# Seven block products for eight in the gate projection of the last four token groups

## The chip, the cores and the metric

The kernel runs on one core of a Trainium2 chip. The metric is device time in microseconds (us) of one execution. Executions of one kernel agree to about 0.3%. No execution here was in a slow state: the granted TensorE clock was between 0.996 and 1.0 in every profiled one. TensorE is called PE in the profile, its weight loads PEld, VectorE DVE, ScalarE ACT, GpSimd POOL and SyncE SP. A profiled span is some 1.8 us shorter than the time of the same execution.

## The reference

Cosine-weighted linear attention over 8 batches, 8 heads, 576 positions and 64 dimensions, then a gated feed-forward block over the resulting 4608 tokens of 512 features:

```python
def _attn_ref(q, k, v):
    # cos_w, sin_w: one number for each position
    def phi(x, c, s):
        r = np.maximum(x, 0.0)
        return np.concatenate([r * c, r * s], axis=-1)
    q_p, k_p = phi(q, cos_w, sin_w), phi(k, cos_w, sin_w)
    kv = np.einsum('bhsf,bhsd->bhfd', k_p, v)
    z = np.sum(k_p, axis=2)
    num = np.einsum('bhsf,bhfd->bhsd', q_p, kv)
    den = np.einsum('bhsf,bhf->bhs', q_p, z)[..., None] + 1e-06
    return num / den

def _moe_ref(x, w_gate, w_val, w_out):      # 4608x512, 512x1536, 512x1536, 1536x512
    g = x @ w_gate
    silu = g * (1.0 / (1.0 + np.exp(-g)))
    val = x @ w_val
    return silu * val @ w_out
```

The change touches `x @ w_gate` only.

## The kernel before

The tokens are handled in nine groups of 512, numbered 0 to 8. A group's projections run chunk by chunk, 12 chunks of 128 of the 1536 hidden features. In each chunk TensorE computes gate and value (4 + 4 products of 512 columns), ScalarE the silu, VectorE the product of the two. TensorE's results go to PSUM, a memory that the kernel handles as eight banks:

```python
    def ffn_mm(tg, fc, lo=0, hi=GH, which=(0, 1)):
        # cut: two PSUM banks, one for gate, one for value
        for i in which:
            for kc in range(KC):        # KC = 4
                nc.tensor.matmul(out=st["f", tg, fc, lo][i], lhsT=(wg_sb, wv_sb)[i][:, kc, fs],
                                 rhs=xT[tg][:, ts, kc], start=(kc == 0), stop=(kc == KC - 1))

    def ffn_silu(tg, fc, ...):
        nc.scalar.activation(out=sg[:, 0:n], in_=st["f", tg, fc, lo][0], func=AF.Silu, scale=DOWN)

    def ffn_mul(tg, fc, ...):
        nc.vector.tensor_tensor(out=ht[:, fc, r:r + n], in0=sg[:, 0:n], in1=ps[1], op=ALU.mult)
```

Behind each chunk stands a slot, into which the attention work for later groups is put: tiles of x of the next group (a TensorE product, then three VectorE steps, then a transposing DMA), table products of queries and values, key-value products. In the traces below VectorE works through its instructions in the order in which the program issues them.

```python
    for t in range(2 * OUT, NTG * OUT):          # tiles of x of groups 2 to 8
        # cut
            at(s, lambda t=t: a_tile2(t), turn(t))   # products, den, rec, x on VectorE; DMA transpose to xT
    for tg in range(1, NTG):
        s0 = SLOTS * tg
        for fc in range(FC):                     # FC = 12 chunks
            ffn_fc(tg, fc)
            if tg > 1:
                sums_behind(fc)                  # sums of tokens for the output, on VectorE
            slot(s0 + fc)
        if tg > 1:
            out_by_quarters(tg, lambda i: slot(s0 + FC + i))
```

`out_by_quarters` is the output projection, and already a block scheme: hidden features and tokens are split in halves, and seven products of half-size blocks stand in for eight, at the price of sums and differences of blocks on VectorE. The key-value result goes from PSUM to SBUF in four copies of one phase, two by ScalarE, two by VectorE:

```python
    def kv_out2(b):
        # cut
        for w, eng in enumerate((nc.scalar.copy, nc.vector.tensor_copy)):
            for i in range(2):
                eng(out=kv2s[b % 2][w * D:(w + 1) * D, :, :, i], in_=ps[i * D:(i + 1) * D, :, :, w])
```

Of the kernel before, what the change touches and what calls it, by code (L numbers as in the profile page):

```python
# [18 lines left out]
def kernel(  # L19
# [10 lines left out]
    nc = tc.nc  # L30
# [17 lines left out]
    HC = FC // 2  # L48
    HT = T // 2
    HD = d_model // 2  # L50

    consts = ctx.enter_context(tc.tile_pool(name="consts", bufs=1))
    raw = ctx.enter_context(tc.tile_pool(name="raw", bufs=3))
    rel = ctx.enter_context(tc.tile_pool(name="rel", bufs=1))
    phip = ctx.enter_context(tc.tile_pool(name="phip", bufs=2))
    xp = ctx.enter_context(tc.tile_pool(name="xp", bufs=4))
    xtp = ctx.enter_context(tc.tile_pool(name="xtp", bufs=3))
    smp = ctx.enter_context(tc.tile_pool(name="smp", bufs=3))
    sgp = ctx.enter_context(tc.tile_pool(name="sgp", bufs=5))
    obp = ctx.enter_context(tc.tile_pool(name="obp", bufs=2))  # L60
    psum = ctx.enter_context(tc.tile_pool(name="psum", bufs=1, space=bass.MemoryType.PSUM))

# [6 lines left out]
    held = {}  # L69

    filled = [False] * 8

    def take(n, hold=None, fills=False, seeded=False):

        taken = {x for r in held.values() for x in r}
        free = [b for b in range(0, 8, n) if not any(b <= x < b + n for x in taken)
                and (filled[b] or not seeded)]

        b0 = min(free, key=lambda b: (n == 1 and hold is not None and hold[0] == "o" and b ^ 1 not in taken,
                                      sorted(used[b:b + n], reverse=True)))  # L80
        if hold is not None:
            held[hold] = range(b0, b0 + n)
        filled[b0:b0 + n] = [fills or seeded] * n
        touch(range(b0, b0 + n))
        return banks[:, b0] if n == 1 else banks[:, b0:b0 + n]
# [15 lines left out]

    def raw_of(b, nm):
        if (b, nm) not in raws:
            raws[b, nm] = raw.tile([P, G, NC, D], BF16, name=f"raw_{nm}")
        return raws[b, nm]

    def load(b, nm, parts=1):
# [48 lines left out]
    ident = consts.tile([P, P], BF16)  # L156
    make_identity(nc, ident)
    kvd = []
    for j in range(2):
        t = consts.tile([P, 8 * J * D1], BF16, name=f"kvd_{j}")  # L160
        if j:
            nc.gpsimd.memset(t.bitcast(FP32), 0.0)
        kvd.append(t.rearrange("p (e j w i x) -> p e j w i x", e=2, j=J, w=2, i=2))


    zeros = consts.tile([P, P], BF16)
# [41 lines left out]
        in_=csk.rearrange("p c e -> p (c e)").to_broadcast([P, NC * 2, D]),  # L208
    )
    v2s = []  # L210
    for j in range(2):
        t = consts.tile([P, G, NC, 2, W], BF16, name=f"v2_{j}")
        nc.vector.tensor_copy(out=t[:, :, :, :, D], in_=csk.unsqueeze(1).to_broadcast([P, G, NC, 2]))
        v2s.append(t)


    wg_sb = consts.tile([P, KC, d_ff], BF16)
    wv_sb = consts.tile([P, KC, d_ff], BF16)
    wg_r = moe_w_gate.rearrange("(c p) f -> p c f", p=P)
    wv_r = moe_w_val.rearrange("(c p) f -> p c f", p=P)  # L220
    wo_r = moe_w_out.rearrange("(c p) f -> p c f", p=P)
# [35 lines left out]

    def vmul(b, g):
        nc.vector.tensor_tensor(  # L259
            out=v2s[b % 2][:, g, :, :, 0:D],  # L260
            in0=(first if b == 0 and g == 0 else {"v": raw_of(b, "v")})["v"][:, g].unsqueeze(2).to_broadcast([P, NC, 2, D]),
            in1=tab, op=ALU.mult,
        )
# [34 lines left out]
    def kv_mm(b):  # L298
        ps = st[b, "kvps"] = take(2, ("kv", b))
        for j, c in [(j, c) for j in range(J) for c in range(NC)]:  # L300
            for i in range(2):
                for e in range(2):
                    es = slice(e * SH, (e + 1) * SH)
                    g = 2 * j + i
                    nc.tensor.matmul(  # L305
                        out=ps[i * D:(i + 1) * D, e, j * 2 * D1:(j + 1) * 2 * D1],
                        lhsT=raws[b, "k"][es, g, c],
                        rhs=v2s[b % 2][es, g, c, :, 0:D1],
                        start=(c == 0), stop=(c == NC - 1),
                    )  # L310

# [47 lines left out]
            give_back(("kvf", j))  # L359


    qf = consts.tile([P, 2, J, 2, D], BF16)
    qr = [lodge(4 * J * SH, BF16).rearrange("p (e j c s) -> p e j c s", e=2, j=J, c=2) for i in range(2)]
    qwT = [lodge(8 * J * SH, BF16).rearrange("p (w e j c s) -> p w e j c s", w=2, e=2, j=J, c=2) for i in range(2)]

# [68 lines left out]
    def x_rec(t, ps, ys=slice(0, 4)):  # L434
        if ys.start == 0:
            st["rec", t] = smp.tile([P, H, 1], FP32, name="rec")
            st["x", t] = xp.tile([P, d_model], BF16, name="x")
        nc.vector.reciprocal(out=st["rec", t].rearrange("p (e y) o -> p e y o", e=2)[:, :, ys],
                             in_=st["den", t].rearrange("p (e y) o -> p e y o", e=2)[:, :, ys])

# [40 lines left out]
    def x_norm(t):  # L481
        num = st.pop(("num", t)).rearrange("p j e (i x) -> p (j e i) x", i=2)
        den = smp.tile([P, H, 1], FP32, name="den")
        nc.vector.tensor_scalar(out=den, in0=num[:, :, D:D1], scalar1=1e-6, scalar2=DOWN,
                                op0=ALU.add, op1=ALU.mult)
        rec = smp.tile([P, H, 1], FP32, name="rec")
        nc.vector.reciprocal(out=rec, in_=den)
        x = xp.tile([P, d_model], BF16, name="x")
        for j in range(J):
            hs = slice(4 * j, 4 * j + 4)  # L490
            nc.vector.tensor_tensor(
                out=x[:, 4 * j * D:(4 * j + 4) * D].rearrange("p (i e d) -> p e i d", i=2, e=2),
                in0=num[:, hs, 0:D].rearrange("p (e i) d -> p e i d", e=2),
                in1=rec[:, hs].rearrange("p (e i) o -> p e i o", e=2).to_broadcast([P, 2, 2, D]), op=ALU.mult,
            )
        st["x", t] = x

    def xT_of(t):
        tg, off = divmod(t, GH // 2)
        if tg not in xT:  # L500
            xT[tg] = xtp.tile([P, GH // 2, KC, P], BF16, name="xT")
        return xT[tg][:, off]

    def x_turn_pe(t, ks=slice(0, KC)):
        ps = take(1, ("xt", t, ks.start)).bitcast(BF16).rearrange("p (k x) -> p k x", x=P)
        for kc in range(ks.start, ks.stop):
            nc.tensor.transpose(out=ps[:, kc], in_=st["x", t][:, kc * P:(kc + 1) * P], identity=ident)  # L507
        st["xt", t, ks.start] = ps[:, ks]

    def x_turned(t, eng, ks=slice(0, KC)):  # L510
# [40 lines left out]
    def ffn_act(*a):  # L551
        ffn_silu(*a)
        ffn_mul(*a)

    def ffn_fc(*a):

        ffn_mm(*a)
        ffn_act(*a)

    out_v = out.rearrange("(b p c) f -> b c p f", p=SH, c=NC)  # L560
    o_ps = {}
# [68 lines left out]
    def out_by_quarters(tg, slot_of):  # L630
# [60 lines left out]
        if last:  # L691
            store_two(t0 + 2, slice(HD, d_model))
        product(c, aq[:, 1, 1], T4, False)
        copied("dve", C21, c)
        free("c")
        if last:
            store_two(t0 + 2, slice(0, HD))
# [175 lines left out]
        load_kv(3)  # L873


    for b in range(2, B):
        s0 = SLOTS * (b - 1)
        keng = "dve" if b == 2 else "act"
        steps = [lambda b=b, g=g: phi_q(b, g) for g in range(G)]
        steps += [lambda b=b, g=g: (relu_k(b, g, g + 1, keng), vmul(b, g)) for g in range(G)]  # L880
        if b == 2:
            fs, tq = [s0 + i for i in (0, 0, 1, 1, 4, 5, 5, 6)], (s0 + 2, s0 + 2)
        else:
            p0 = s0 - SLOTS
            fs, tq = [p0 + 12, p0 + 12] + [p0 + 11 + i for i in range(2, 8)], (p0 + 15, p0 + 16)
            if b == 3:
                fs, tq = [p0 + 12 + i for i in range(4)] + [s0 + 4, s0 + 4, s0 + 5, s0 + 5], (s0 + 2, s0 + 2)
            at(p0 + 3 if b < 5 else p0 + 1, lambda b=b: load_behind(b))
        tk = (s0 + 4, s0 + {2: 8, 3: 7}.get(b, 5))
        for s, f in zip(fs, steps):  # L890
            at(s, f)
        for e in range(2):
            at(tq[e], lambda b=b, e=e: qturn_dma(b, e))
        at(tk[-1], lambda b=b: kv_mm(b), lambda b=b: kv_out2(b))
        at(tk[-1] + 1, lambda b=b: kv_free(b))
    for t in range(2 * OUT, NTG * OUT):
        tg, i = divmod(t, OUT)
        s = SLOTS * (tg - 1) + (5 if tg > 2 else 4) + 2 * i
        if t == 2 * OUT:
            at(s, a_(t, 0))  # L900
            at(s + 1, a_(t, 1), turn(t))
        elif tg == 2:
            at((9, 10, 11)[i - 1] + SLOTS, lambda t=t: a_tile2(t), turn(t))
            if i == 2:
                at(11 + SLOTS, load_3)
        else:
            if t in (13, 14, 15):
                s = SLOTS * 2 + t - 4
            at(s, lambda t=t: a_tile2(t), turn(t))
    for tg in range(1, NTG):  # L910
        s0 = SLOTS * tg
        for fc in range(FC):
            ffn_fc(tg, fc)
            if tg > 1:
                sums_behind(fc)
# [3 lines that stand above are left out]
            continue  # L919
        for i in range(OUT):  # L920
            ffn_out(tg * OUT + i)
            weight_sum(i)
            slot(s0 + FC + i)
# [31 lines left out]
```

## Time and profile before

| | before |
|---|---|
| time, median of the 4 runs beside the changed kernel | 318.05 us (317.81 to 318.79) |
| profiled span | 316.2 us |
| busy: TensorE / VectorE / ScalarE | 309.1 / 220.2 / 134.1 us |
| group 5, from its first gate product to that of group 6 | 32.39 us |
| group 6 / group 7, in the same way | 32.43 / 30.92 us |
| group 8, projections / output to the end of the span | 20.72 / 13.96 us |

The prediction below shows the lines of the page and the table of stretches. One more view is needed: the waits of TensorE by cause. Each line names the waiting engine, tile and line, what it waited for, then the microseconds in total, the number of times and the longest.

```profile
PE banks L172 <- DVE zeros L167: 1.0, 1, 1.0
PE banks L401 <- DVE wt_sb L389: 0.6, 1, 0.6
PE banks L376 <- DVE qf L368: 0.4, 1, 0.4
PE banks L535 <- DMA xT<-x: 0.2, 1, 0.2
```

Three of the four are at the start of the program; from the steady groups on there is one wait of 0.2 us. There is no idle time of TensorE left to remove, only work.

### The profile page before, as it was taken

To read this page: it belongs to the slowest core of one execution; us is meant where nothing else is said; L and a number is where in the kernel's file an instruction comes from. 1 tells how busy PE (TensorE), PEld (TensorE's weight loads), DVE (VectorE), ACT (ScalarE), POOL (GpSimd) and SP (SyncE) were. 2 spreads that over 40 slices of the span, in tenths; PEclk is the share of its full clock that TensorE was granted. 3 is DMA by queue.
4 is the path that set the end of the run, shared out by engine and by line. 5 is a ranking of instruction groups with operands and counts; after the bars stand their busy time and mean duration, and the time that the engine had idled before them with its cause. 6 is when DMAs were issued, how large, how long until landed. Compare 5 with 4: busy or idle time off the path is not lost.

```text
span 316.2 us, 6614 instructions
## 1 busy us (share of the span) xinstructions
PE 309.1 (98%) x2624; PEld 182.7 (58%) x2624; DVE 220.2 (70%) x441; ACT 134.1 (42%) x245; POOL 35.5 (11%) x60
## 2 busy tenths in 40 slices
PE   8899999999999999999999999999999999999994
PEld 4596555455445485548554765477456745774473
DVE  7873777797658888597858785879578437743652
ACT  7554545753435354335433453344433133213330
POOL 6754102000201100030003000300000000000000
PEclk9999999999999999999999999999999999999999
DMA  7999999998796985979795979598951241133004
GB/s 259 220 198 197 206 205 139 226 130 110 140 225 88 175 116 135 129 80 197 148 142 75 200 149 145 72 199 134 157 77 35 58 93 23 39 69 72 2 0 133
DMA packets 74766, 41.06 MB, mean 130 GB/s; under 512 B 49904, under 2 KB 69872, under 8 KB 74736
## 3 DMA queue, kind: packets, MB, share of 16 engines
q1 hardware_dynamic: 51952, 22.55, 39.7%
q0 software_dynamic: 22192, 17.57, 37.1%
q10 hardware_dynamic: 592, 0.52, 0.5%
q8 instruction: 20, 0.33, 0.4%
q14 instruction: 10, 0.08, 0.1%
HBM read 37.75 MB, written 9.44 MB: 149 GB/s over the span
## 4 chain that ended last, share of the span: by engine, by line
PE 86%; DVE 6%; DMA 4%; ACT 2%; issue 1%; DVEq 0%; ACTq 0%
PE banks L535 57%; PE banks L649 15%; PE banks L592 6%; DMA xT<-x 4%; PE banks L305 3%; PE banks L419 2%; DVE ht L546 1%; DVE sums L623 1%; DVE x L442 1%; PE banks L465 1%; PE banks L401 1%; DVE v L259 1%; PE banks L172 1%; PE banks L345 0%; PE banks L507 0%
## 5 line engine op out<-in xcount | busy, mean ns | idle before, releaser
L541 ACT ACTIVATE sg<-banks 128x512 bf16<-128x512 f32 (+2 forms) x116 | 65.8, 568 | 118.7 <-PE banks L535 115.6
L535 PE MATMUL banks<-xT,wg_sb 128*128 128x512 bf16 (+2 forms) x464 | 111.3, 364 | 0.3 <-DMA xT<-x 0.2
L535 PE MATMUL banks<-xT,wv_sb 128*128 128x512 bf16 (+2 forms) x464 | 111.3, 364 | 0.0
L546 DVE TENSOR_TENSOR ht<-sg,banks 128x512 f16<-128x512 bf16 (+2 forms) x116 | 74.5, 648 | 52.2 <-PE banks L535 45.5
L535 PEld LDWEIGHTS <-wv_sb 128*128 128x128 bf16 x464 | 44.9, 98 | 48.7
L535 PEld LDWEIGHTS <-wg_sb 128*128 128x128 bf16 x464 | 43.0, 98 | 42.3 <-issue 0.4
L649 PEld LDWEIGHTS <-ht 128*128 128x128 f16 x336 | 32.4, 98 | 3.9
L649 PEld LDWEIGHTS <-sums 128*128 128x128 f16 x252 | 24.6, 98 | 3.6 <-issue 0.8
L259 DVE TENSOR_TENSOR v<-raw_v,tab 128x1152 bf16<-128x1152 bf16 x31 | 22.7, 751 | 0.3 <-ACT raw_v L712 0.3
L592 PE MATMUL banks<-wo_sb,ht 128*128 128x512 f16 x96 | 22.7, 379 | 0.0
L442 DVE TENSOR_TENSOR x<-banks,rec 128x512 bf16<-128x512 f32 (+1 forms) x32 | 21.6, 674 | 1.3 <-PE banks L401 0.3
L649 PE MATMUL banks<-wo_sb,ht 128*128 128x256 f16 x168 | 20.6, 273 | 0.0
L649 PE MATMUL banks<-wt_sb,sums 128*128 128x256 f16 x168 | 19.5, 273 | 0.0
L649 PE MATMUL banks<-wt_sb,ht 128*128 128x256 f16 x168 | 19.5, 273 | 0.0
L255 DVE TENSOR_TENSOR r_q<-raw_q,tab 128x1152 bf16<-128x1152 bf16 x24 | 17.6, 752 | 2.4 <-ACT raw_q L238 2.1
L238 ACT ACTIVATE raw_k<-raw_k 128x576 bf16<-128x576 bf16 (+1 forms) x25 | 17.0, 694 | 0.0
L861 POOL COPY hold<-phit 1x2 bf16<-1x2 bf16 x5 | 1.2, 234 | 130.4 <-DMA phit<-r_q 130.4
L623 DVE TENSOR_TENSOR sums<-ht 128x1024 f16<-128x1024 f16 (+1 forms) x28 | 15.5, 552 | 0.2
L238 ACT ACTIVATE raw_q<-raw_q 128x576 bf16<-128x576 bf16 x24 | 15.0, 674 | 0.0
L592 PEld LDWEIGHTS <-ht 128*128 128x128 f16 x96 | 9.1, 98 | 8.9 <-issue 0.2
L419 PEld LDWEIGHTS <-phit 128*128 128x128 bf16 (+1 forms) x240 | 10.0, 100 | 6.5 <-issue 1.3
L664 DVE TENSOR_SCALAR ob<-banks 128x512 f32<-128x512 f32 (+1 forms) x15 | 9.8, 656 | 4.4 <-PE banks L649 3.6
(98 smaller groups left out, 223.9 us busy)
## 6 DMA issues: line engine op xcount, KB each, us to landing
out_dram<-ob SPq DMA_DIRECT2D x67, 128.0 KB, 2.4
raw_k<-in_k_dram POOLq DMA_DIRECT2D x7, 576.0 KB, 9.0
raw_q<-in_q_dram POOLq DMA_DIRECT2D x6, 576.0 KB, 6.5
raw_v<-in_v_dram POOLq DMA_DIRECT2D x6, 576.0 KB, 11.7
wo_sb<-in_moe_w_out_dram POOLq DMA_DIRECT2D x3, 512.0 KB, 12.8
wg_sb<-in_moe_w_gate_dram POOLq DMA_DIRECT2D x5, 256.0 KB, 9.0
wv_sb<-in_moe_w_val_dram POOLq DMA_DIRECT2D x5, 256.0 KB, 9.3
wo_sb<-in_v_dram SPq DMA_DIRECT2D x2, 576.0 KB, 4.1
```

The source lines that it names most:

```text
L238: nc.scalar.activation(out=out, in_=in_, func=AF.Relu)
L255: nc.vector.tensor_tensor(out=st[b, "q"][:, g], in0=o.unsqueeze(2).to_broadcast([P, NC, 2, D]), in1=tab, op=ALU.mult)
L259: nc.vector.tensor_tensor(out=v2s[b % 2][:, g, :, :, 0:D], in0=(first if b == 0 and g == 0 else {"v": raw_of(b, "v")})["v"][:, g].unsqueez ...
L419: nc.tensor.matmul(out=ps[ms, e, g * D1:(g + 1) * D1], lhsT=phit[b][:, e, g, c:c + n].rearrange("p c s -> p (c s)"), rhs=kv2s[b % 2][:, e, ...
L442: nc.vector.tensor_tensor(out=st["x", t].rearrange("p (y e d) -> p e y d", e=2, d=D)[:, :, ys], in0=ps[:, :, 0:2 * J * D1].rearrange("p e ...
L535: nc.tensor.matmul(out=st["f", tg, fc, lo][i], lhsT=(wg_sb, wv_sb)[i][:, kc, fs], rhs=xT[tg][:, ts, kc], start=(kc == 0), stop=(kc == KC - 1))
L541: nc.scalar.activation(out=sg[:, 0:n], in_=st["f", tg, fc, lo][0], func=AF.Silu, scale=DOWN)
L546: nc.vector.tensor_tensor(out=ht[:, fc, r:r + n], in0=st.pop(("s", tg, fc, lo))[:, 0:n], in1=ps[1], op=ALU.mult)
L592: nc.tensor.matmul(out=o_ps[t], lhsT=ht[:, fc, r:r + P], rhs=wo_sb[:, fc], start=(fc == 0), stop=(fc == FC - 1))
L623: nc.vector.tensor_tensor(out=o[:, lo:hi], in0=x[:, lo:hi], in1=y[:, lo:hi], op=op)
L649: nc.tensor.matmul(out=to[i][:, 0] if len(to) == 2 else to[0][:, i], lhsT=a[:, kc, i * P:(i + 1) * P], rhs=b[:, kc], start=first and kc == ...
L664: nc.vector.tensor_single_scalar(out=o_, in_=p_, scalar=x, op=ALU.mult)
```

## The change

The intent is to apply to the gate projection of groups 5 to 8 what the output projection does already: seven block products for eight. The gate weights are split into A11, A12 (odd chunks; first and second half of the 512 features) and A21, A22 (even chunks), x by features and tokens into B11 to B22. Each of three column blocks `u` covers four chunks. Weight differences W1 to W4 are made once, differences of x (X1 to X4) once a group, and the results are put together in PSUM: `a` and `b` are accumulators, `b` starts as ScalarE's copy of `a`, and VectorE makes two sums with a PSUM operand in each block. Values keep their full products, which are put between the block products. The core, with cuts:

```diff
+    GATE = (5, 6, 7, 8)
     def take(n, hold=None, fills=False, seeded=False):   # choice of a PSUM bank
+        if loose[0]:
+            # one bank: the oldest, but first those that leave a free pair; two: the oldest pair
-    raw = ctx.enter_context(tc.tile_pool(name="raw", bufs=3))
+    raw = ctx.enter_context(tc.tile_pool(name="raw", bufs=2))        # keys and values
+    rawq = ctx.enter_context(tc.tile_pool(name="rawq", bufs=3))
-    wg_sb = consts.tile([P, KC, d_ff], BF16)     # likewise wv_sb, x, xT
+    wg_sb = consts.tile([P, KC, d_ff], FP16)
+    def x_sum(tg, n):
+        B11, B12, B21, B22 = x_parts(tg)
+        o, x, y = ((X1, B12, B11), (X2, B22, X1), (X3, B22, B12), (X4, B21, X2))[n]
+        nc.vector.tensor_tensor(out=o, in0=x, in1=y, op=ALU.subtract)
+    def ffn_by_quarters(tg, slot_of):
+        # product(): 4 matmuls of 256 columns; V(): the 4 value products; mul(): gate times value
+        for u in range(3):
+            product(a, u, A11, B11, True)
+            nc.scalar.copy(out=b, in_=a)
+            product(e, u, W3, X3, True)
+            nc.scalar.copy(out=m7, in_=e)
+            V(...);  done()                       # done() is the slot
+            product(b, u, W2, X2, False)
+            nc.vector.tensor_tensor(out=c, in0=m7, in1=b, op=ALU.add)
+            product(a, u, A12, B21, False);  silu(u, 1, 0, a)
+            # if u: mul of the block before
+            V(...);  done()
+            product(b, u, W1, X1, False)
+            nc.vector.tensor_tensor(out=m7, in0=m7, in1=b, op=ALU.add);  silu(u, 0, 1, m7)
+            product(c, u, A22, X4, False);  silu(u, 0, 0, c)
+            V(...);  done()
+            mul(u, 0, 0);  mul(u, 1, 0)
+            product(b, u, W4, B22, False);  silu(u, 1, 1, b)
+            # V, mul, and a slot if u
-        copied("dve", C21, c)                     # one output copy, VectorE to ScalarE
+        copied("act", C21, c)
+    for n in range(4):
+        at(SLOTS * (1 + n * (GATE[0] - 1) // 4) + FC + 3, lambda n=n: gate_weight_sum(n))
+    for tg in GATE:
+        for n in range(4):
+            at(SLOTS * (tg - 1) + FC + (2, 2, 3, 3)[n], lambda tg=tg, n=(2, 0, 1, 3)[n]: x_sum(tg, n))
+            elif tg - 1 in GATE:                  # slots of the tiles of x
+                s = SLOTS * (tg - 1) + ((1, 2, 7, 9) if tg < 6 else (1, 2, 4, 7) if tg < 8 else (1, 2, 5, 6))[i]
```

The sums of x come first in their slots: they are put into the plan ahead of the attention work of the same slot. They lie in the space of the doubled key-value buffer of the first batches, the weight differences in that of a doubled value product.

> **What bounds the kernel now.** I read the page's busy line, then the chain that ended last, then a table of stretches (one per group of 512 tokens), then the engines in order of time around the start of group 5.
>
> ```profile
> PE 309.1 (98%) x2624; PEld 182.7 (58%) x2624; DVE 220.2 (70%) x441; ACT 134.1 (42%) x245; POOL 35.5 (11%) x60
> ...
> PE 86%; DVE 6%; DMA 4%; ACT 2%; issue 1%; DVEq 0%; ACTq 0%
> PE banks L535 57%; PE banks L649 15%; PE banks L592 6%; DMA xT<-x 4%; PE banks L305 3%; PE banks L419 2%; DVE ht L546 1%; DVE sums L623 1%; DVE x L442 1%; PE banks L465 1%; PE banks L401 1%; DVE v L259 1%; PE banks L172 1%; PE banks L345 0%
> ...
> L535 PE MATMUL banks<-xT,wg_sb 128*128 128x512 bf16 (+2 forms) x464 | 111.3, 364 | 0.3 <-DMA xT<-x 0.2
> L546 DVE TENSOR_TENSOR ht<-sg,banks 128x512 f16<-128x512 bf16 (+2 forms) x116 | 74.5, 648 | 52.2 <-PE banks L535 45.5
> ```
>
> TensorE is the bound: 86% of the chain, and almost no idle time ahead of the gate products (0.3 us). A product removed there is worth its whole slot, as long as nothing else ends up in front of TensorE. The stretches, with TensorE, weight-load, VectorE and ScalarE busy time, for groups 5, 6, 7 and 8 (the last split into projections and output):
>
> ```profile
> 185.70:218.10 32.40, 32.29 (x284) 19.61 (x285) 24.56 (x46) 14.25 (x25) 2.70 (x4) 1.00 0.90 141
> 218.10:250.60 32.50, 32.50 (x295) 19.70 (x293) 22.20 (x43) 11.40 (x20) 0.00 (x0) 1.00 0.50 86
> 250.60:281.50 30.90, 30.90 (x214) 18.63 (x212) 18.55 (x36) 8.94 (x15) 0.00 (x0) 1.00 0.24 52
> 281.50:302.20 20.70, 20.70 (x98) 9.42 (x97) 10.79 (x17) 7.18 (x12) 0.00 (x0) 1.00 0.23 51
> ```
>
> The reader is to see that VectorE has 24.6 of 32.4 us taken in group 5, 22.2 in group 6, 18.6 of 30.9 in group 7 and 10.8 of 20.7 in group 8: spare time is scarce just where the change starts, and plentiful at the end. TensorE and VectorE around the start of group 5:
>
> ```profile
> 184.14 1.47 PE L649 MATMUL banks<-wo_sb,sums 128*128 128x256 f16 x12
> 185.78 1.02 PE L535 MATMUL banks<-xT,wg_sb 128*128 128x512 bf16 x4 [0.17 <-DMA xT<-x]
> 186.64 1.03 PE L535 MATMUL banks<-xT,wv_sb 128*128 128x512 bf16 x4
> ...
> 178.05 0.69 DVE L442 TENSOR_TENSOR x<-banks,rec 128x512 bf16<-128x512 f32 x1
> 183.41 0.68 DVE L690 SCALAR_TENSOR_TENSOR ob<-banks,ob 128x512 f32<-128x512 f32 x1
> 184.76 0.75 DVE L255 TENSOR_TENSOR r_q<-raw_q,tab 128x1152 bf16<-128x1152 bf16 x1
> 185.65 0.69 DVE L664 TENSOR_SCALAR ob<-banks 128x512 f32<-128x512 f32 x1
> ```
>
> Four products of 512 columns start every 0.86 us (185.78 to 186.64). The last x of group 5 leaves VectorE at 178.74 and its transposed copy lands at about 185.65 (the chain has 6.88 us of DMA there), so TensorE waits 0.17 us for it: the DMA is already just on time.
>
> **What the Trainium skill says.** "TensorE: Matmul & The Clock Gate", section "Wait — 56ns, not 53.3ns?", gives a warm matmul as N / 2.4 GHz plus about 2.5 ns from start to start. The trace agrees: the output's products, 12 of 256 columns, start 1.31 us apart as a set (from 176.09 to 177.40 in group 4), 109 ns each, and 864 / 4 = 216 ns for 512 columns; so half-width products cost almost exactly half. "VectorE: DVE Perf Modes", section "The perf-mode tier table", lets tensor_tensor run at 2x on 16-bit SBUF data and at 1x with a PSUM operand. The trace agrees: 1024 fp16 elements from SBUF take 684 ns, 512 take 421, and 512 with a PSUM operand take 685. So each new add on a PSUM bank is as dear as a gate-times-value product. "PSUM — Partial Sum Buffer", section "The four PSUM rules", says that VectorE and ScalarE writes neither set nor clear the written-bits, so a matmul without the first flag accumulates on them where an earlier matmul set the bit; that is why the change keeps track of filled and seeded banks. The output projection does this already, without a stall in the trace.
>
> **The change part by part.**
> - TensorE, removed: 12 chunks x 4 products x 216 ns = 10.37 us of gate per group. Added: 3 column blocks x 7 block products x 4 matmuls of 256 columns x 109.2 ns = 9.17 us. Saved 1.19 us a group, 4.8 us for four groups (1.5% of the time). This is the ceiling.
> - ScalarE, added per group: 6 copies (bank to bank, bank to SBUF) of about 0.57 us (the output's same copy), and one 0.60 us output copy moved from VectorE: 4.0 us. It has 14.3 of 32.4 us busy in the fullest group: room enough.
> - VectorE, added per group: 6 adds with a PSUM operand, 6 x 0.69 = 4.1 us; 4 sums of x of 512 fp16, 4 x 0.42 = 1.7 us; less one 0.69 us output copy. Net 5.1 us. Once each at the end of groups 1 to 4: a weight sum of 1536 fp16, 0.95 us.
> - VectorE after the change, on the records: group 5 24.6 + 5.1 = 29.7 us of a possible 31.2 (32.4 - 1.19), and one weight sum at its start; group 6 27.3 of 31.2; group 7 23.6 of 29.7; group 8 16 in 19.5. Records overlap: back to back, ops recorded at 0.69 start 0.60 apart, so the real load in group 5 is nearer 26 us. It fits on average, but the adds are in a chain: TensorE may not add to the accumulator b again before VectorE has read it.
>
> The chain within one column block, on TensorE alone: b's second product ends 2.17 us into the block, the add that reads it can be done at about 3.1, and b's third product is due at 3.47. The margin is 0.4 us, and the next add has the same. Anything that VectorE does between (a tile of x: 0.16 + 0.20 + 0.69 us, 1.03 from start to next start; a value-times-table product of 0.75 us) goes straight into TensorE's wait. I walked each group by hand with the instruction order of the changed program and the durations above:
> - Group 5. The sums of x stand in VectorE's order ahead of the last query product and output copy, and the first two need the copy that lands at 185.65. From there: 2 sums (0.34 apart), query product 0.73, output copy 0.60, weight sum 0.86, then the third sum, done at about 189.0. The third block product needs it and is due at 187.5: 1.5 us lost. Two table products (0.73 each) then stand ahead of the first add: 0.5 us more. In the second and third column block the bank of product e is one that a late tile of x or a gate-times-value product still holds, and the latter stands behind the key-value copies, which wait for ScalarE's (1.2 us of VectorE idle in the trace of before): 0.9 + 0.8 us, and about 1 us in small waits. Full count near 4.8 us, less 1.2 saved.
> - Group 6: the same without the DMA wait and the weight sum: about 2.5 us, less 1.2.
> - Group 7: no table products, no key-value copies: 0.9 us at most, less 1.2.
> - Group 8: no attention work: waits under 0.1 us, the full 1.2 saved. The output at its end finds its last token sum about 0.3 us ahead of need (0.75 before).
>
> Full count of the waits: 8.3 us against 4.8 saved, which would be 321.5. Such a hand count takes every delay at its worst order, and small errors in latencies of 0.1 us decide several of these waits, so I take some 60% of it, 5.0 us: 317.99 - 4.8 + 5.0 = 318.2.
>
> **Rivals.**
> 1. The saving comes through almost whole (waits of 1 to 2 us in all): 314.5 to 315. For it: the output projection of the same form runs its 84 products in 9.2 us without a gap, the page's mean load of VectorE is 70%, and the slots of the tiles were plainly moved to make room. Against it: 29.7 of 31.2 us in group 5, and a transposed copy that lands 6.9 us after its x.
> 2. VectorE becomes the bound in groups 5 and 6 as counted: 320 to 322. For it: the walk. Against it: an author who had seen 3 us lost in group 5 would have started one group later.
> 3. Buffers: key and value loads have two buffers for three, and the doubled value product one for two. The loads are issued on a transposed query, 28 to 34 us after the one before, long after the batch two back was used; hidden, 0 us. Extra identity at the start: 0.5 us on GpSimd, which then waits 1.8 us for the first load anyway; 0 us.
> 4. More weight loads (84 for 48 a group): 98 ns each beside 109 ns of product, and the output runs in this regime with no gap; 0 us.
>
> **Range and chances.** Predicted 318.2 us. Rival 1 sets the lower end, 314.3; rival 2 the upper, 321.7. Faster by over 2% needs 311.6, below the ceiling of 313.2: 0.01. Slower by over 2% needs 324.4, which is 11 us of waits: 0.05. Within 2%: 0.94.
>
> **What would show each step.** Right: gate products of 256 columns in sets of four 0.44 us apart in group 8, and groups 7 and 8 shorter by 0.3 to 1.2 us; VectorE about 20 us busier over the span; in group 5 a wait of TensorE over 1 us on a sum of x, and in groups 5 and 6 waits of TensorE on VectorE's adds and tiles of x, from nearly none before. Wrong: groups 5 and 6 shorter than before (rival 1), or TensorE's waits on DMA or ScalarE rather than VectorE. If group 8 isn't about 1.2 us shorter, the count of products itself is wrong.

## The result, and the profile after

| | before | after |
|---|---|---|
| median of 4 runs each | 318.05 us | 321.14 us (320.99 to 321.82) |
| ratio after / before | | 1.0097, 95% interval 1.0075 to 1.012 |

Ratios here and below are the mean time of one kernel's fast runs over that of the other's of the same rounds, so they are not quite the ratio of the quoted medians. The changed kernel is 1.0% slower. TensorE has less arithmetic to do, and the kernel takes longer.

Its page, busy times and then the shares of the chain that ended last:

```profile
PE 307.3 (96%) x2768; PEld 196.8 (61%) x2768; DVE 238.1 (74%) x478; ACT 149.1 (47%) x276; POOL 36.1 (11%) x62
...
PE 82%; DVE 11%; ACT 3%; issue 2%; DMA 1%; DVEq 0%; ACTq 0%
```

VectorE has 17.9 us more (238.1 - 220.2), and its share of the chain went from 6% to 11%. The stretches, each from the first gate product of a group to that of the next (the last: group 8's projections). The columns are those of the prediction's table: the length, then busy time and instructions of TensorE, weight loads, VectorE, ScalarE and GpSimd, the granted clock, the DMA share and GB/s.

```profile
185.15:221.85 36.70, 32.60 (x322) 23.11 (x320) 30.52 (x59) 17.71 (x33) 2.41 (x4) 1.00 0.79 124
221.85:255.76 33.91, 32.32 (x330) 23.16 (x328) 26.77 (x52) 15.21 (x28) 0.00 (x0) 1.00 0.47 83
255.76:286.52 30.76, 30.38 (x250) 22.12 (x248) 22.87 (x45) 12.22 (x22) 0.00 (x0) 1.00 0.24 52
286.52:306.05 19.53, 19.53 (x134) 12.91 (x132) 13.65 (x23) 9.77 (x18) 0.00 (x0) 1.00 0.23 55
```

Set against before, with the 1.19 us that each group's products save:

| stretch | before | after | difference | lost to waits (difference + 1.19) | counted in the prediction |
|---|---|---|---|---|---|
| group 5 | 32.39 | 36.70 | +4.31 | 5.5 | 4.8 |
| group 6 | 32.43 | 33.91 | +1.48 | 2.7 | 2.5 |
| group 7 | 30.92 | 30.76 | -0.16 | 1.0 | 0.9 at most |
| group 8, projections | 20.72 | 19.53 | -1.19 | 0.0 | under 0.1 |
| group 8, output | 13.96 | 13.95 | -0.01 | | |

Group 5 starts 0.63 us earlier than before, so the four differences of the groups, less 0.63, give the 3.8 us between the spans. This profiled execution was the slowest of its four (321.82 us), for a reason that comes below.

The waits of TensorE after:

```profile
PE banks L621 <- DVE kvt L605: 2.3, 2, 1.3
PE banks L621 <- DVE x L471: 1.6, 3, 0.7
PE banks L621 <- DVE ht L638: 1.3, 2, 0.6
...
PE banks L621 <- DVE banks L659: 0.2, 1, 0.2
```

L621 is the block product; `kvt` is the space that holds the sums of x (L605 makes them), `x` a tile of x, `ht` a gate-times-value product, `banks` at L659 the first sum with a PSUM operand. All are VectorE's. TensorE in group 5 in order of time, the first set, the sets ahead of which it was idle, and one of value products between; the bracket has the idle time and what ended it:

```profile
185.15 0.60 PE L621 MATMUL banks<-xT,wg_sb 128*128 128x256 f16 x4
186.71 0.60 PE L621 MATMUL banks<-kvt,wgs_sb 128*128 128x256 f16 x4 [0.96 <-DVE kvt L605]
187.15 1.03 PE L633 MATMUL banks<-xT,wv_sb 128*128 128x512 f16 x4
189.52 0.61 PE L621 MATMUL banks<-kvt,wgs_sb 128*128 128x256 f16 x4 [1.35 <-DVE kvt L605]
...
191.92 0.60 PE L621 MATMUL banks<-kvt,wgs_sb 128*128 128x256 f16 x4 [0.23 <-DVE banks L659]
...
195.92 0.60 PE L621 MATMUL banks<-kvt,wgs_sb 128*128 128x256 f16 x4 [0.68 <-DVE x L471]
...
204.76 0.60 PE L621 MATMUL banks<-kvt,wgs_sb 128*128 128x256 f16 x4 [0.63 <-DVE ht L638]
```

Five waits, 3.85 us of idle time, where the group lost 5.5. The starts show the rest. A set of four with 256 columns is recorded at 0.60 us, but where nothing holds it up the next set starts 0.44 us after it (286.52 and 286.96, below), and one of 512 columns is recorded at 1.03 with the next 0.86 us after it. The last 0.16 us of a record overlap with the next one, so each wait costs 0.16 us more than its bracket says: the third product starts 2.37 us after the value products at 187.15, where 0.86 would do, and has lost 1.51. From start to start the five are 1.12, 1.51, 0.39, 0.84 and 0.79 us, 4.65 in all. Four delays that the view doesn't bracket add 0.83: 0.30 at 194.21 (it follows the second sum with a PSUM operand), 0.16 at 205.36, 0.25 at 208.46 (the first such sum of the last column block) and 0.12 in the output's set of 24 from 213.67. Together that is 5.48.

What VectorE did meanwhile, at the start of the group:

```profile
186.23 0.76 DVE L605 TENSOR_TENSOR kvt<-xT 128x512 f16<-128x512 f16 x2 [2.44 <-DMA xT<-x]
186.91 0.75 DVE L283 TENSOR_TENSOR r_q<-raw_q,tab 128x1152 bf16<-128x1152 bf16 x1
187.58 0.68 DVE L801 TENSOR_SCALAR ob<-banks 128x512 f32<-128x512 f32 x1
188.18 0.95 DVE L597 TENSOR_TENSOR wgs_sb<-wg_sb,wgs_sb 128x1536 f16<-128x1536 f16 x1
189.05 0.87 DVE L605 TENSOR_TENSOR kvt<-xT,kvt 128x512 f16<-128x512 f16 x2
189.84 1.42 DVE L287 TENSOR_TENSOR v<-raw_v,tab 128x1152 bf16<-128x1152 bf16 x2
```

The reader is to see a queue in which the urgent stands behind the leisurely. VectorE is idle for 2.44 us, because the next entry in its order is a sum of x whose transposed copy has not landed. It then makes two sums, but the third, which TensorE needs next, stands behind a query's table product, an output copy and a weight difference, none of which TensorE waits for yet: 2.1 us from 186.91 to 189.05. The Trainium skill, page "TensorE: Matmul & The Clock Gate", section "Architectural detail: the array is 16× 32×32, not 1× 128×128", calls the queues of ScalarE and VectorE "strict FIFO". The trace agrees: the third sum's operands had all been there since 187.0 (the parts of x, and X1, which is one of the first two sums, done 0.76 us after 186.23), yet it began at 189.05.

Group 8 has none of this. Its sets follow one another with no wait, 4 x 109 ns apart as the count assumed (286.52, 286.96, 287.39):

```profile
286.52 0.60 PE L621 MATMUL banks<-xT,wg_sb 128*128 128x256 f16 x4
286.96 0.60 PE L621 MATMUL banks<-kvt,wgs_sb 128*128 128x256 f16 x4
287.39 1.03 PE L633 MATMUL banks<-xT,wv_sb 128*128 128x512 f16 x4
```

### The profile page after: what moved, and what is told of

Its sections match the earlier page's. It is cut to its first block, busy times and chain, and to the rows that moved or that the text cites. A ratio compares the mean times of both kernels' runs of the same rounds, so it can differ in the third digit from the quotient of the medians.

```text
span 320.0 us, 6926 instructions
## 1 busy us (share of the span) xinstructions
PE 307.3 (96%) x2768; PEld 196.8 (61%) x2768; DVE 238.1 (74%) x478; ACT 149.1 (47%) x276; POOL 36.1 (11%) x62
## 4 chain that ended last, share of the span: by engine, by line
PE 82%; DVE 11%; ACT 3%; issue 2%; DMA 1%; DVEq 0%; ACTq 0%
PE banks L564 33%; PE banks L786 20%; PE banks L633 9%; PE banks L621 7%; PE banks L729 6%; DVE x L471 2%; PE banks L448 2%; DVE v L287 2%; PE banks L333 2%; DVE ht L638 1%; DVE banks L659 1%; PE banks L494 1%; DVE m L668 1%; DVE rec L467 1%; PE banks L430 1%
## 5 line engine op out<-in xcount | busy, mean ns | idle before, releaser
L570 ACT ACTIVATE sg<-banks 128x512 bf16<-128x512 f32 (+2 forms) x68 | 37.2, 547 | 53.4 <-PE banks L564 51.3
L564 PE MATMUL banks<-xT,wg_sb 128*128 128x512 f16 (+2 forms) x272 | 62.0, 354 | 0.0
L564 PE MATMUL banks<-xT,wv_sb 128*128 128x512 f16 (+2 forms) x272 | 62.0, 354 | 0.0
L575 DVE TENSOR_TENSOR ht<-sg,banks 128x512 f16<-128x512 bf16 (+2 forms) x68 | 41.6, 621 | 22.5 <-PE banks L564 15.5
L633 PE MATMUL banks<-xT,wv_sb 128*128 128x512 f16 x192 | 48.6, 379 | 0.0
L564 PEld LDWEIGHTS <-wv_sb 128*128 128x128 f16 x272 | 26.1, 98 | 26.1
L564 PEld LDWEIGHTS <-wg_sb 128*128 128x128 f16 x272 | 25.0, 98 | 21.8
L638 DVE TENSOR_TENSOR ht<-sg,banks 128x512 f16<-128x512 bf16 x48 | 31.0, 680 | 2.5 <-ACT sg L627 2.4
L621 PEld LDWEIGHTS <-wgs_sb 128*128 128x128 f16 x192 | 18.0, 97 | 15.2 <-issue 6.9
L633 PEld LDWEIGHTS <-wv_sb 128*128 128x128 f16 x192 | 18.8, 98 | 13.7 <-issue 0.5
L621 PE MATMUL banks<-kvt,wgs_sb 128*128 128x256 f16 x144 | 21.6, 272 | 5.8 <-DVE kvt L605 2.3
L471 DVE TENSOR_TENSOR x<-banks,rec 128x512 f16<-128x512 f32 (+1 forms) x32 | 21.6, 674 | 1.3 <-PE banks L430 0.3
```

The source lines that it names most:

```text
L471: nc.vector.tensor_tensor(out=st["x", t].rearrange("p (y e d) -> p e y d", e=2, d=D)[:, :, ys], in0=ps[:, :, 0:2 * J * D1].rearrange("p e ...
L575: nc.vector.tensor_tensor(out=ht[:, fc, r:r + n], in0=st.pop(("s", tg, fc, lo))[:, 0:n], in1=ps[1], op=ALU.mult)
L621: nc.tensor.matmul(out=to[:, i], lhsT=a[:, c, 2 * u + i], rhs=x[:, :, c], start=first and i == 0 and c == 0, stop=c == KH - 1, skip_group_ ...
L633: nc.tensor.matmul(out=val[u, i, w], lhsT=wv_sb[:, kc, fc * P:(fc + 1) * P], rhs=xT[tg][:, :, kc], start=(kc == 0), stop=(kc == KC - 1))
L638: nc.vector.tensor_tensor(out=ht[:, fc], in0=gates[u, w][:, i], in1=val.pop((u, i, w)), op=ALU.mult)
```

## The experiments

The theory: each group pays its products' saving plus waits for VectorE's order, which grow with the attention work that lies in the group. Rival A: something else in the change (fp16, the buffers, the bank choice, the moved output copy) costs the time. Rival B: the block products save less than counted. Rival C: VectorE has simply too much to do, whatever the order (the later expectations call this rival D). All kernels below were timed in five rounds against the kernel before, whose medians were 318.25 us (the first four), 318.27 (the next four) and 318.54 (the last four, on another chip); so ratios are compared, and 0.001 in a ratio is 0.32 us. The intervals are about 0.0013 to either side, and that of the changed kernel's own ratio is 0.0023, so a difference against the changed kernel is uncertain by some 0.8 us. All results but one were correct.

One build failed before these: gate products with the old choice of banks. The record doesn't hold it. Built again while this text was checked, with all four groups, it stops in group 6: a tile of x asks for two neighbouring banks, and the old choice, which takes aligned pairs alone, finds none free. So with four groups the change needs the new choice. With `GATE = (8,)` or `(7, 8)` the old choice does build; none of the runs times that.

### Which group pays: four rungs of a ladder

e1, the change without the block products, and so also without their sums, the new slots of the tiles and the new choice of banks, which the code switches on with the first gate group:

```diff
-    GATE = (5, 6, 7, 8)
+    GATE = ()
-    for n in range(4):
-        at(SLOTS * (1 + n * (GATE[0] - 1) // 4) + FC + 3, lambda n=n: gate_weight_sum(n))
```

> No group by seven products: all the rest of the change alone (fp16 x and weights, two key/value buffers, one doubled value buffer, shared tiles, one output copy on ScalarE, new tile slots of group 5 unchanged). Theory (VectorE's order makes TensorE wait in groups 5 and 6): as before, 318.0 within 0.3 us, since the trace of the changed kernel starts group 5 no later than before. Rival A (the rest costs): 319.5 to 321.

Measured: 317.79 us, ratio 0.9987 (0.9975 to 0.9999). What it keeps (fp16, the buffers, the moved output copy) costs nothing, and perhaps gives 0.4 us. For these rival A falls. The new choice of banks is not in e1, and every kernel with block products has it; it stays untested by itself. In e2, below, block products and bank choice together lose 0.1 us, which is within the noise.

e2, block products in group 8 alone: `GATE = (8,)`.

> Only group 8 by seven products. Theory: 1.05 us faster than before (1.19 of products less 0.14 of wait at the output's sums), 317.0. Rival B (a block product costs more than half a product, for its weight loads or starts): slower by a quarter of the loss, 318.8.

Measured: 316.79 us, ratio 0.9952 (0.9939 to 0.9965). Against e1 that is 0.0035, 1.1 us, for 1.19 counted. Rival B falls.

e3, groups 7 and 8: `GATE = (7, 8)`.

> Groups 7 and 8. Theory: group 7 gains 0.2 us (in the changed kernel 30.76 for 30.92), so 316.8. Rival B: 319.5. Rival C (VectorE's load is over its limit wherever there is attention work): group 7 loses, 317.5 or more.

Measured: 316.91 us, ratio 0.9959 (0.9944 to 0.9974). Group 7 brings nothing, 0.2 us of loss within the noise where 0.2 of gain was expected.

e4, groups 6 to 8: `GATE = (6, 7, 8)`.

> Groups 6 to 8. Theory: group 6 loses 1.5 us (33.9 for 32.4) without the DMA wait of group 5, perhaps 0.5 more for the weight sum that now stands at its start: 318.3 to 318.8. If group 6 was only late from group 5: 317 or less.

Measured: 318.5 us, ratio 1.0009 (0.9995 to 1.0022). Group 6 costs 0.0050, 1.6 us; and group 5, the step from here to the changed kernel, 0.0088, 2.8 us. The ladder by ratios, with 1.19 us added to each step, gives waits of about 0.1, 1.4, 2.8 and 4.0 us for groups 8, 7, 6 and 5: 8.3 us in all, each uncertain by some 0.5, that of group 5 by 0.8. (The expectation has the fourth weight difference at the start of group 6; in e4's profile it is at 186.38 us, at the start of group 5, as in the changed kernel.)

### Which waits in group 5: three single repairs

e5 makes the second, third and fourth weight differences one group earlier. The fourth moves from 188.2 to 154.0 us, so that it doesn't stand ahead of the third sum of x:

```diff
-        at(SLOTS * (1 + n * (GATE[0] - 1) // 4) + FC + 3, lambda n=n: gate_weight_sum(n))
+        at(SLOTS * (1 + n * (GATE[0] - 2) // 4) + FC + 3, lambda n=n: gate_weight_sum(n))
```

> The last weight sum (0.95 us of VectorE) moved from the start of group 5 to the end of group 3; nothing removed. Theory (order at a tight spot): third block product of group 5 starts 0.87 us earlier, 320.3. Rival D (VectorE's total load over groups 5 and 6 is the limit, order doesn't matter): the work is only moved out of a stretch that starts with an idle wait for DMA anyway; unchanged, 321.1.

Measured: 320.5 us, ratio 1.0068 (1.0054 to 1.0081), 0.9 us under the changed kernel: one operation of 0.95 us is gone from the start of group 5, and its start-to-start time of 0.87 us came back, with an uncertainty as large as itself. The profile is plainer. The wait on the third sum fell by just 0.87, from 1.35 to 0.48 us:

```profile
186.28 0.60 PE L621 MATMUL banks<-kvt,wgs_sb 128*128 128x256 f16 x4 [0.20 <-DVE kvt L605]
188.22 0.61 PE L621 MATMUL banks<-kvt,wgs_sb 128*128 128x256 f16 x4 [0.48 <-DVE kvt L605]
```

e6 turns the last tile of group 5 on TensorE, with ScalarE's copy, in place of the DMA transpose that lands late:

```diff
-            at(s, lambda t=t: a_tile2(t), turn(t))
+            if t == 23:
+                at(s, lambda t=t: a_tile2(t))
+                at(SLOTS * (tg - 1) + FC, turn(t, True))
+            else:
+                at(s, lambda t=t: a_tile2(t), turn(t))
```

> The last tile of x for group 5 is transposed by TensorE (4 transposes, some 0.22 us) and copied by ScalarE in place of the DMA that lands at 186.2. Theory: the waits of 0.96 and 1.35 us ahead of group 5's sums fall to some 0.4 in all, 0.5 remains at the first add: 2.1 less 0.2, 319.2. Rival D: 320.8 or more.

Measured: 320.15 us, ratio 1.0065 (1.005 to 1.0079), 1.0 us under the changed kernel: half of what was expected. The cause is the reading of one profile. The first wait on a sum of x is 0.96 us in the profiled execution of the changed kernel, but 0.20 us in e5's, above, and 0.24 in e7's, where nothing was done about it. The landing of that DMA varies between executions, the profiled one was the slowest of its four, and 0.7 us of what e6 was to remove is not there in most runs. From the start of the last x on VectorE to the first instruction that waits for its copy, it is 7.5 to 7.8 us in seven profiles (before, e2, e3, e4, e5, e7, e9) and 8.5 in two (the changed kernel and e12). Group 5 without it has lost some 4.8 us, not 5.5.

No run tried to make the copy land earlier, though the trace of before has a hint. The eight transposes of x issued during groups 6 and 7 land 2.4 to 2.9 us after their issue; the last three for group 5 take 6.7 to 8.2. These were issued at 170.8 to 178.8, close to three loads of 576 KB each of queries, keys and values (issued at 170.65 to 172.11, the last landed at 185.20). That the loads hold up the copies is likely, but not shown; issuing them later would test it.

e7 gives all four key-value copies of batches 6 and 7 to ScalarE:

```diff
-        for w, eng in enumerate((nc.scalar.copy, nc.vector.tensor_copy)):
+        for w, eng in enumerate((nc.scalar.copy, nc.scalar.copy if b >= 6 else nc.vector.tensor_copy)):
```

> In groups 5 and 6 all four key-value copies on ScalarE, so VectorE doesn't wait for ScalarE's pair. Theory: the wait of 0.63 us ahead of product e in the third column block goes, with the 0.16 after it, in both groups: 1.6 to 1.7 us, 319.5. If the wait only changes its cause (the later adds are late anyway): 320.8.

Measured: 319.53 us, ratio 1.0038 (1.0026 to 1.005), 1.9 us under the changed kernel. The two waits on `ht` of 0.63 us, one each in groups 5 and 6, are gone from its list. In the changed kernel VectorE stood idle for 1.93 us ahead of its copies, which waited for ScalarE's own to end; three gate-times-value products stood behind them:

```profile
203.13 0.87 DVE L356 CAST kv<-banks 64x260 bf16<-64x260 f32 x2 [1.93 <-ACT kv L356]
204.02 1.88 DVE L638 TENSOR_TENSOR ht<-sg,banks 128x512 f16<-128x512 bf16 x3
```

The Trainium skill, page "Perfetto Trace Analysis", section "Optimizing Scalar/DVE Operations", says that where VectorE is saturated, giving work to ScalarE may make sense. It did here, although VectorE was idle just ahead of the copies: what was saved was the wait in its queue, not only the 0.87 us of work.

e8 has all three repairs.

> The three edits together, all four groups by seven products. Theory: 2.6 less 0.2 in group 5's start and 1.7 at the two key-value copies: 317.0. What is left would be the 0.7 us waits on a late tile of x in groups 5 and 6. Rival D: 319.5 or more.

Measured: 317.42 us, ratio 0.9972 (0.9957 to 0.9987): 0.28% faster than before with all four groups, correct result. Against the changed kernel that is 0.0125, 4.0 us, where the three alone sum to 3.8. Within the noise the three gains add up.

### Load or order

e9 takes the value table products of batches 6 and 7 away altogether (the result is wrong on purpose, with a relative error of 0.77):

```diff
     def vmul(b, g):
+        if b >= 6:
+            return
```

> The changed kernel without the eight value-times-table products that VectorE runs at the start of groups 5 and 6 (batches 6 and 7; the result is wrong on purpose). 2.7 us of VectorE less in each group. Theory (only what stands in front of a tight spot counts): the waits at the first add (0.23), the second (0.3) and on the tile of x (0.68) go in each group, those on the sums of x and behind the key-value copies stay: 1.2 us a group, 318.7. Rival D (the load as such): 2.7 us a group, 315.7.

Measured: 319.3 us, ratio 1.0021 (1.0009 to 1.0033), 2.4 us under the changed kernel, as the theory had it (1.2 us a group), for eight operations of 0.67 us from start to start, 5.4 us of VectorE. If VectorE's load alone were the bound (rival C), the whole should have come back. What remains is what stands in the wrong place:

```profile
189.10 0.61 PE L623 MATMUL banks<-kvt,wgs_sb 128*128 128x256 f16 x4 [1.35 <-DVE kvt L607]
194.48 0.60 PE L623 MATMUL banks<-kvt,wgs_sb 128*128 128x256 f16 x4 [0.35 <-DVE x L473]
203.32 0.60 PE L623 MATMUL banks<-kvt,wgs_sb 128*128 128x256 f16 x4 [0.63 <-DVE ht L640]
```

The third sum's wait (1.35) and that behind the key-value copies (0.63) are untouched; the sum with a PSUM operand no longer waits (0.23 before), and the tile's wait went from 0.68 to 0.35. Moving one 0.95 us operation (e5) was worth 0.9 us; removing eight was worth 0.3 us each.

### Moving the tiles: a theory that fell

What e8 had left was the wait on a tile of x, 0.67 us in each of groups 5 and 6: the bank that product `e` takes is still held by a tile. e10 and e11 are e8 with the tiles moved to other slots in all gate groups:

```diff
-                s = SLOTS * (tg - 1) + ((1, 2, 7, 9) if tg < 6 else (1, 2, 4, 7) if tg < 8 else (1, 2, 5, 6))[i]
+                s = SLOTS * (tg - 1) + (1, 4, 6, 8)[i]     # e11: (1, 4, 7, 8)
```

> The three edits together with the tiles of x in slots 1, 4, 6, 8 for 1, 2, 4, 7 (1, 2, 5, 6 in group 7), so that product e of the second column block no longer takes the bank of a tile that was just issued. Theory: waits of 0.67 in groups 5 and 6 and 0.3 in group 7 go, some of it comes back at the adds: 1.2 us, 316.2. If the lateness only moves on: 317.4.

> As the run before with slots 1, 4, 7, 8: the third tile ahead of the first add of the last column block (1.0 us of VectorE there), as in the changed kernel: 316.3; the two should differ by less than 0.5 us.

Measured: e10 320.14 us, ratio 1.0047 (1.0035 to 1.0059); e11 319.08 us, ratio 1.0013 (1.0001 to 1.0025). A gain was expected, and e10 is 2.4 us slower than e8, e11 1.3 us. The waits on tiles did go away as foreseen. The waits of e10, without those from the start of the program:

```profile
PE banks L621 <- DVE m L668: 1.3, 4, 0.4
...
PE banks L786 <- DVE sums L760: 1.0, 3, 0.3
PE banks L621 <- ACT banks L649: 0.7, 2, 0.4
```

New ones took their place: on the second sum with a PSUM operand (`m`), on the token sums that the output needs (0.33 us in every group), on ScalarE's copies. Groups 5 and 7 of e8, and then of e10, in the table of stretches:

```profile
186.00:219.03 33.03, 31.95 (x322) 23.15 (x320) 28.03 (x54) 18.23 (x35) 2.41 (x4) 1.00 0.92 138
...
252.00:282.76 30.76, 30.39 (x250) 22.14 (x248) 22.88 (x45) 12.21 (x22) 0.00 (x0) 1.00 0.24 52
```

```profile
185.85:219.80 33.95, 32.31 (x323) 23.09 (x321) 28.21 (x54) 18.33 (x35) 2.41 (x4) 1.00 0.84 135
...
253.67:285.17 31.50, 30.58 (x250) 22.11 (x248) 22.69 (x45) 12.11 (x22) 0.00 (x0) 1.00 0.23 51
```

They are 0.92 and 0.74 us longer in e10, and group 6 is 0.90 us (32.97 to 33.87), though VectorE's busy time is the same within 0.2 us. So the same work in another order is 2.6 us slower in that pair of profiles, which speaks once more against rival C. Where it comes from shows in VectorE's own waits in e10's group 5:

```profile
193.33 1.88 DVE L638 TENSOR_TENSOR ht<-sg,banks 128x512 f16<-128x512 bf16 x3 [0.52 <-ACT sg L627]
195.58 0.70 DVE L659 TENSOR_TENSOR banks<-m,banks 128x512 f32<-128x512 f32 x1 [0.37 <-ACT m L653]
```

With a tile less between 193 and 196, VectorE is idle there for 0.9 us; in e8 it was making that tile. The tile comes later, at 206.4, among the sums for the output, and those end at 213.4 rather than 212.7. Time once idle isn't given back: the old slots filled a hole in VectorE's order, the new ones left it open and made the end late. Counted from start to start as above, TensorE's delays in group 5 sum to 3.09 us in e10 and to 2.17 in e8, which is the whole difference.

e11 differs from e10 by one slot of one tile, and was expected to be within 0.5 us of it; it is 1.1 us better. Its groups 5 and 6 lack two delays that e10 has at the start of the last column block, at 202.22 and 202.94 in group 5: product `e` waits for a silu, then the value products for a gate-times-value product (0.16 and 0.13 us idle, 0.32 and 0.29 from start to start). In e10 a tile takes two banks just ahead of them, at 201.20; that the choice of banks makes the difference is a guess.

e12 is e3 with the same move, `GATE = (7, 8)` and tiles at (1, 4, 6, 8).

> Only groups 7 and 8 by seven products, tiles of x in slots 1, 4, 6, 8. Theory: group 7 loses its wait of 0.3 us: 316.6. Without any wait in group 7 it would be 316.0.

Measured: 317.28 us, ratio 0.9958 (0.9947 to 0.9969): the same as e3's 0.9959. The 0.3 us wait on a tile is gone from its list, and 0.5 us on `m` and 0.3 us on the token sums are there for it.

The best of all is e2 with group 8 alone, 0.48% faster than before, or e3 with 7 and 8, 0.41%; the intervals do not tell the two apart.

## Why the prediction was right or wrong

The time fell within the range (321.14 of 314.3 to 321.7), near its upper end, and in the class held likeliest. The predicted point, 318.2, was 2.9 us low, and the range held only because it reached up to the full count of waits that the text itself had marked down. By its steps:

- **Products saved, 1.19 us a group.** Right to the digit where nothing else moved: group 8's projections are 1.19 us shorter, and e2 by itself gained 1.1 us.
- **VectorE's added work.** Predicted to be about 20 us over the span, measured 17.9; the prediction's own items add up to 24 (4 x 5.1 and 4 x 0.95), so the 20 leaves out the weight sums. ScalarE's, 4.0 us a group or 16, measured 15.0 (149.1 - 134.1). Group 5's VectorE time was foreseen at 29.7 us plus a weight difference; it is 30.5.
- **Which waits.** Right, one by one, and in size too when they are measured as they were counted, from start to start in group 5: the third sum of x counted 1.5, measured 1.51; the first sum with a PSUM operand 0.5 against 0.39; the bank of product `e` 0.9 against 0.84; behind the key-value copies 0.8 against 0.79; small waits about 1 against 0.83. One was missed: the first sum of x, which waits for the landing, 0.2 us of idle time in e5's and e7's profiles and 0.96 in the changed kernel's. e5 shortened one of these waits, e7 removed another in two groups, and each gained what it should.
- **The size of the waits in sum: here the prediction failed.** The full count was 8.3 us, which gives 321.5 us. The text then took "some 60% of it", 5.0 us, because a hand count "takes every delay at its worst order". By the clock the waits are 321.14 - 318.05 + 4.76 = 7.9 us; by the ladder of e1 to e4, 8.3; by the stretches of the one profile, 5.5 + 2.7 + 1.0 = 9.2, of which 0.7 is the late landing of that execution and 0.63 is made up by the earlier start of group 5, so 7.9 again. The term that was mis-sized is this discount. There was nothing to discount: VectorE kept the program's order, as the traces show, so the counted order was not the worst one but the only one, and the single waits came out as counted.
- **Rival 2.** Its number was right, 320 to 322; its words, that VectorE becomes the bound, only in part: in e9 and e10 its order decides, not its load alone. The argument against it was that an author who had seen 3 us lost in group 5 would have started one group later. It says nothing of the chip, and the ladder shows that starting one group later is better by 2.8 us, and three groups later by 4.6.
- **Rivals 1, 3 and 4.** The first fell. That the output projection of the same form runs without gaps was no good precedent: it has two sums with a PSUM operand in a group, where the gate blocks have six (a likely reason, not tested). The third held: e1 shows no cost of buffers. The fourth held too: group 8 runs 84 weight loads for 48 without a gap.

What stays open: how much of the wait for the bank of product `e` (0.84 us in groups 5 and 6 and 0.46 in group 7, from start to start) the new choice of banks makes, how e11 comes to be better than e10, and why the last copy of x lands late.

## What to carry to other kernels

When TensorE is the bound and another engine is to take on small sums in return for fewer products, the spare time of that engine is not the whole question: the rest is whether each sum can be made in the gap between the product that feeds it and the product that needs it, given what stands ahead of it in that engine's order. Walk through the order with the durations of the trace, measure waits from start to start, and don't mark the sum down. It is no proof either: for e10 a forecast of the same kind was wrong by 3.6 us (1.2 gained expected, 2.4 lost). Try the change first in the stretch where the helping engine is idle: here the last group alone gained as much as the four groups with three repairs, and more.

## What the Trainium skill lacked or had wrong

- "DMA: Bandwidth & Descriptors", section "DMA Transpose (X-bar)": its constraints are given, but no time from issue to landing for one SBUF-to-SBUF transpose, and nothing on its spread; the one time that another page gives is for a 128x128 block. In the kernel before, 30 such transposes took 2.4 to 9.7 us, with a median of 3.0, and the one that TensorE waits for at the start of group 5 took 6.9. The wait for it was 0.28 us in e3's profile and 0.89 us in e12's, two kernels that are the same up to there, on two chips.
- "Perfetto Trace Analysis", section "Identifying the Most-Contended Engine": the engine with the highest occupancy is to be optimised first. The page has no measure of how much of a second engine may be taken before the first one stalls on its order. Here TensorE lost 5.5 us a group with VectorE 83% busy (30.52 of 36.70 us), 2.7 with 79%, 1.0 with 74% and nothing with 70%; and at one and the same load (28.0 and 28.2 us in group 5) two orders differed by 0.9 us.
- "VectorE: DVE Perf Modes", section "The DRAIN you can't avoid", says that the next operation does not start until the pipe has emptied, though it points to cases in which it starts earlier. It doesn't say how this looks in a profile. Where no wait stands between them here, the next record starts before the last one ends: operations recorded at 0.68 to 0.69 us with a PSUM operand have the next start 0.60 us after their own (188.18 after 187.58), and a 0.95 us one 0.87 us after (189.05 after 188.18). Whether the pipe is empty by then the runs don't tell. Adding up the durations of single records overstates VectorE's load by about a tenth.
